# A new hand-written step order for a fused linear-attention and gated-FFN kernel: the same steps, another list

## The chip, the cores and the metric

The kernel runs on one core of one Trainium2 chip. The metric is the device time of one execution in microseconds, the median of several executions. The engines are TensorE (PE, with its weight loads shown as PEld), VectorE (DVE), ScalarE (ACT), GpSimd (POOL) and SyncE (SP, which issues DMAs).

## The reference

Eight batches of 8 heads, 576 tokens and 64 channels go through a linear attention, and the 4608 resulting rows of 512 channels go through a gated FFN, all in float32 at the interface.

```
q_s = exp(q - max(q over channels));  q_s /= sum(q_s) + 1e-9      # per token
k_s = exp(k - max(k over tokens));    k_s /= sum(k_s) + 1e-9      # per channel
kv  = einsum('bhsd,bhse->bhde', k_s, v)
x   = einsum('bhsd,bhde->bhse', q_s, kv)      # then laid out as [4608, 512]
out = ((x @ w1) * (x @ w2)) @ w3 @ w_out      # w1, w2: 512x1024; w3: 1024x1024; w_out: 1024x512
```

## The kernel before

The product w3 @ w_out is formed once on the chip ("fold"), so that the FFN is two up-projections, a product, and one down-projection with the folded matrix W3O. All matmuls are in float16 with float32 accumulation. Each batch b gives 512 rows to chunk b of the FFN and 64 rows to a ninth chunk (c = 8), the tail. The first two chunks are cut into two halves of 256 rows so that the FFN can start earlier.

The whole program is a set of named steps. `Plan.add` registers a step with the engine or engines that may run it; `Plan.run` goes through one text, `ORDER`, and emits the steps in exactly that order. Nothing is scheduled after that: each engine executes its own steps in the order in which the text names them, and semaphores hold a step until what it reads is there and the buffer that it writes is free. Where a step may run on more than one engine, the letter behind the slash chooses (A is ACT, D is DVE, P is POOL). The list is the only thing that the change touches.

The steps by name, with b the batch, c the chunk, u one of the parts of the 1024 hidden columns:

- Loads: `q.b`, `k.b`, `v.b`, `w1`, `w2`, `w3`, `wo`. Those of the first two batches and the weights are issued from POOL, except q.0; the others from SP. The loads fill buffers that alternate between two, so a load of batch b waits for the last reader of batch b-2. The first of SP's later loads, `q.2`, also waits for the landing of the load `w1.1` (the gate).
- Fold: `w3t` (8 transposes on PE), `w3T` (a copy out of PSUM), `pf` (8 matmuls in two halves), `W3O` (scaled copy). There are eight of each.
- Keys: `kmx` and `cb` (column maximum, DVE), `ksub` (POOL or DVE), `kexp` (ACT), `vc` (cast of v, POOL or ACT), `kv` (PE, 72 small matmuls), `kv2` (DVE: add epsilon, reciprocal, two multiplications out of PSUM; lines L461, L462 and L464).
- Queries: `qmx` (DVE), `qsub` (POOL or DVE), `qexp` (ACT), `qsm` (row sum, DVE, L512), `qeps` (add epsilon, ACT at L518 or DVE at L519), `qrc` (reciprocal, DVE, L523), `qn` (POOL or DVE), then `qd` (a transposing DMA issued from SP, L564), or for batch 0 `qt` and `qT` through PE.
- Attention output: `xm` (the 512 rows) and `xt` (the 64 tail rows) on PE, L582, from `kv2` and the transposed q; `xs` and `xts` scale them out of PSUM into the FFN's input x.
- FFN: `up.1` and `up.0` on PE (L726), `bs` (copy of the first product, ACT or DVE), `ab` (the elementwise product, DVE, L741), `down` on PE (L748, in the tail L763), `os` (copy out, ACT or DVE) and `st` (store, SP).
- `zero` steps: one keeps 13 matmuls of zeros on PE at the start, and the others 1, 3 or 6 by their code.

PSUM is eight banks used in rotation: a step that takes a bank waits until the copy (`bs`, `ab`, `os`, `xs`, `kv2`...) of the step that had it eight takes earlier is through. `kv`, `xm` and `xt` take two banks each.

The chain of small steps for one half p of a batch's queries reads, in the code:

```
A(("qsm", b, p), "DVE", lambda p=p: qsm(p), ...
A(("qeps", b, p), MOVES, lambda eng, p=p: qeps(p, eng), [summed], port=True, size=n1 - n0)
A(("qrc", b, p), "DVE", lambda p=p: qrc(p), [("qeps", b, p)], size=n1 - n0)
```

so that `qrc` on DVE waits for `qeps`, which may be on ACT, which waits for `qsm` on DVE.

Of the kernel before, what the change touches and what calls it, by code (L numbers as in the profile page):

```python
# [78 lines left out]
up.0.1.0.1 qsub.2.1/P up.1.1.0.2 up.0.1.0.2 bs.1.0.1/A qrc.2.0 ab.1.0.1 qexp.2.1 qsm.2.1 v.2 vc.2.1/P vc.2.0/P  # L79
bs.1.0.2/A xt.0 xts.0.1/A ab.1.0.2 xts.0.0/D qd.1.1 xm.1.1 up.1.1.0.3 qn.2.0/P up.0.1.0.3 xs.1.1.0/A  # L80
qeps.2.1/A qrc.2.1 qn.2.1/P k.3 st.0.3 xs.1.1.1/A up.1.1.1.0 up.0.1.1.0 up.1.1.1.1 kmx.2.1 cb.2 q.3 bs.1.0.3/A
bs.1.1.0/A ab.1.1.0 bs.1.1.1/A up.0.1.1.1 ab.1.1.1 up.1.1.1.2 bs.1.1.2/A st.0.0 ab.1.0.3 qd.2.1 ksub.2.1/P
kexp.2.1 up.0.1.1.2 down.1.0 up.1.1.1.3 up.0.1.1.3 kmx.3.0 qmx.3.0 st.0.1 os.1.0/A ab.1.1.2 qmx.3.1 ksub.2.0/P
kexp.2.0 bs.1.1.3/A down.1.1 os.1.1/A ab.1.1.3 kv.2 qsub.3.0/P qsub.3.1/P qexp.3.0 down.1.2 os.1.2/A kv2.2
qd.2.0 xm.2.1 xs.2.1.0/A xm.2.0 xs.2.0.1/A xs.2.0.0/A down.1.3 qsm.3.0 kmx.3.1 xs.2.1.1/A up.1.2.0.0
up.0.2.0.0 up.1.2.0.1 v.3 cb.3 vc.3.0/P ksub.3.0/P qeps.3.0/A qexp.3.1 os.1.3/A bs.2.0.0/A qsm.3.1 ab.2.0.0
ksub.3.1/P qeps.3.1/A qrc.3.1 up.0.2.0.1 up.1.2.0.2 up.0.2.0.2 up.1.2.0.3 up.0.2.0.3 up.1.2.0.4 up.0.2.0.4
bs.2.0.1/A bs.2.0.2/A q.4 qmx.4.0 ab.2.0.1 kexp.3.0 ab.2.0.2 qmx.4.1 bs.2.0.3/A ab.2.0.3 qn.3.1/P qrc.3.0
qn.3.0/P qsub.4.0/P qsub.4.1/P bs.2.0.4/A k.4 ab.2.0.4 st.1.0 kexp.3.1 kmx.4.1 q.5 v.4 st.0.2 st.1.3 vc.4.1/P
up.1.2.0.5 up.0.2.0.5 up.1.2.0.6 bs.2.0.5/A vc.3.1/A ab.2.0.5 bs.2.0.6/A up.0.2.0.6 ab.2.0.6 xt.1 qd.3.1  # L90
qd.3.0 kmx.4.0 xts.1.0/A kv.3 up.1.2.0.7 bs.2.0.7/A up.0.2.0.7 st.1.1 k.5 qexp.4.0 qexp.4.1 xts.1.1/A v.5 q.6
ab.2.0.7 down.2.0 os.2.0/A kv2.3 cb.4 st.2.0 st.1.2 qmx.5.1 qsm.4.0 down.2.1 down.2.2 xm.3.0 xs.3.0.1/D
os.2.1/A os.2.2/A xm.3.1 xs.3.1.1/A xs.3.0.0/A xs.3.1.0/A down.2.3 os.2.3/A qsm.4.1 qmx.5.0 up.1.3.0.0 kmx.5.1
qeps.4.1/A qrc.4.1 bs.3.0.0/A up.0.3.0.0 ksub.4.1/P qeps.4.0/A ksub.4.0/P ab.3.0.0 up.1.3.0.1 up.0.3.0.1
up.1.3.0.2 bs.3.0.1/A ab.3.0.1 qrc.4.0 qsub.5.1/P vc.4.0/P kexp.4.0 kexp.4.1 k.6 up.0.3.0.2 up.1.3.0.3
bs.3.0.3/A bs.3.0.2/A kmx.5.0 cb.5 ab.3.0.2 up.0.3.0.3 ab.3.0.3 up.1.3.0.4 up.0.3.0.4 up.1.3.0.5 bs.3.0.4/A
bs.3.0.5/A vc.5.0/A qexp.5.1 up.0.3.0.5 ab.3.0.5 ab.3.0.4 up.1.3.0.6 bs.3.0.6/A up.0.3.0.6 up.1.3.0.7 ab.3.0.6
vc.5.1/A xt.2 qn.4.1/P qn.4.0/P qsub.5.0/P kv.4 qd.4.0 qd.4.1 xts.2.1/A bs.3.0.7/A qexp.5.0 kv2.4 up.0.3.0.7
ab.3.0.7 down.3.0 qmx.6.0 ksub.5.1/P ksub.5.0/P os.3.0/A kexp.5.1 kexp.5.0 xts.2.0/D qsm.5.0 qsm.5.1 q.7
down.3.1 qeps.5.0/A os.3.1/A qrc.5.0 qeps.5.1/D down.3.2 os.3.2/A xt.3 xts.3.0/A xts.3.1/A kmx.6.1 qrc.5.1  # L100
kv.5 kv2.5 xm.4.1 xs.4.1.0/A kmx.6.0 cb.6 xm.4.0 xs.4.0.0/A xs.4.0.1/A down.3.3 xs.4.1.1/A up.1.4.0.0
up.0.4.0.0 up.1.4.0.1 bs.4.0.1/A bs.4.0.0/A up.0.4.0.1 up.1.4.0.2 qn.5.0/P ab.4.0.0 qmx.6.1 st.2.1 v.6 st.2.3
st.3.0 st.2.2 k.7 qd.5.0 qn.5.1/P qsub.6.0/P qexp.6.0 st.3.1 qd.5.1 os.3.3/A qmx.7.0 st.3.2 up.0.4.0.2
up.1.4.0.3 up.0.4.0.3 bs.4.0.3/A ab.4.0.3 ab.4.0.1 bs.4.0.2/D ab.4.0.2 up.1.4.0.4 up.0.4.0.4 up.1.4.0.5
bs.4.0.5/D up.0.4.0.5 bs.4.0.4/A ab.4.0.4 v.7 st.3.3 up.1.4.0.6 bs.4.0.6/A up.0.4.0.6 up.1.4.0.7 up.0.4.0.7
ab.4.0.6 ab.4.0.5 bs.4.0.7/D ab.4.0.7 down.4.0 down.4.1 ksub.6.1/P qsub.6.1/P qexp.6.1 qsm.6.1 kmx.7.1
kexp.6.1 ksub.6.0/P kexp.6.0 os.4.0/D os.4.1/A down.4.2 os.4.2/A st.4.2 st.4.0 st.4.1 xt.4 xts.4.1/A qmx.7.1
vc.6.1/P vc.6.0/P qeps.6.1/A xts.4.0/A qrc.6.1 qsub.7.0/P qn.6.1/P kv.6 xm.5.1 xm.5.0 xs.5.0.0/D kv2.6
xs.5.0.1/A xs.5.1.1/A down.4.3 xs.5.1.0/A up.1.5.0.0 up.0.5.0.0 up.1.5.0.1 up.0.5.0.1 up.1.5.0.2 os.4.3/A
bs.5.0.1/A qsub.7.1/P bs.5.0.2/A kmx.7.0 cb.7 qsm.6.0 qeps.6.0/A qexp.7.0 up.0.5.0.2 up.1.5.0.3 bs.5.0.0/D  # L110
up.0.5.0.3 ab.5.0.2 up.1.5.0.4 ab.5.0.0 qrc.6.0 bs.5.0.3/A ab.5.0.3 ab.5.0.1 qexp.7.1 bs.5.0.4/A ksub.7.0/P
vc.7.0/P qn.6.0/P ksub.7.1/P kexp.7.1 up.0.5.0.4 ab.5.0.4 qd.6.0 qd.6.1 up.1.5.0.5 bs.5.0.5/D up.0.5.0.5
up.1.5.0.6 bs.5.0.6/D up.0.5.0.6 ab.5.0.6 ab.5.0.5 up.1.5.0.7 up.0.5.0.7 bs.5.0.7/D ab.5.0.7 down.5.0 down.5.1
qsm.7.1 qsm.7.0 os.5.0/D kexp.7.0 xm.6.1 xs.6.1.1/A xm.6.0 down.5.2 down.5.3 os.5.1/A qeps.7.1/A xs.6.1.0/D
qrc.7.1 qeps.7.0/D xs.6.0.0/D xt.5 xt.6 qrc.7.0 xts.5.1/D xts.6.1/D os.5.3/D xts.5.0/D xs.6.0.1/A vc.7.1/A
kv.7 kv2.7 os.5.2/A up.1.6.0.0 bs.6.0.0/D up.0.6.0.0 ab.6.0.0 up.1.6.0.1 bs.6.0.1/D xts.6.0/A up.0.6.0.1
ab.6.0.1 up.1.6.0.2 up.0.6.0.2 up.1.6.0.3 st.5.1 up.0.6.0.3 qn.7.1/P qd.7.1 qn.7.0/P qd.7.0 st.5.3 st.4.3
st.5.0 bs.6.0.2/D ab.6.0.2 bs.6.0.3/D ab.6.0.3 xm.7.1 xs.7.1.0/A xm.7.0 xs.7.0.1/D xs.7.1.1/A xs.7.0.0/A xt.7
xts.7.1/D up.1.6.0.4 up.0.6.0.4 up.1.6.0.5 bs.6.0.4/A ab.6.0.4 bs.6.0.5/A up.0.6.0.5 up.1.6.0.6 up.0.6.0.6
ab.6.0.5 xts.7.0/D bs.6.0.6/D ab.6.0.6 up.1.6.0.7 up.0.6.0.7 up.1.7.0.0 bs.6.0.7/A ab.6.0.7 down.6.0 down.6.1  # L120
up.0.7.0.0 bs.7.0.0/A os.6.1/A up.1.7.0.1 down.6.2 ab.7.0.0 bs.7.0.1/D down.6.3 os.6.0/D os.6.3/D os.6.2/A
st.6.0 st.6.1 st.5.2 st.6.2 up.0.7.0.1 up.1.7.0.2 up.0.7.0.2 up.1.7.0.3 ab.7.0.1 bs.7.0.2/D ab.7.0.2
up.0.7.0.3 up.1.7.0.4 bs.7.0.3/D up.0.7.0.4 up.1.7.0.5 up.0.7.0.5 ab.7.0.3 bs.7.0.4/D ab.7.0.4 bs.7.0.5/D
ab.7.0.5 up.1.7.0.6 up.0.7.0.6 up.1.7.0.7 bs.7.0.6/D ab.7.0.6 bs.7.0.7/A up.0.7.0.7 ab.7.0.7 down.7.0 down.7.1
down.7.2 os.7.2/A st.7.2 os.7.0/D os.7.1/D st.7.1 st.6.3 up.1.8.0.0 up.0.8.0.0 bs.8.0.0/D ab.8.0.0 up.1.8.0.1
bs.8.0.1/D up.0.8.0.1 up.1.8.0.2 ab.8.0.1 up.0.8.0.2 up.1.8.0.3 bs.8.0.2/A ab.8.0.2 up.0.8.0.3 up.1.8.0.4
up.0.8.0.4 bs.8.0.4/D ab.8.0.4 up.1.8.0.5 up.0.8.0.5 bs.8.0.3/D bs.8.0.5/A ab.8.0.3 up.1.8.0.6 bs.8.0.6/A
up.0.8.0.6 up.1.8.0.7 ab.8.0.6 bs.8.0.7/D up.0.8.0.7 ab.8.0.7 ab.8.0.5 down.7.3 os.7.3/D st.7.3 st.7.0
# [741 lines left out]
```

## Time and profile before

| | before |
|---|---|
| median of 3 runs | 235.85 us (235.81 to 236.25) |
| the profiled execution's own time | 236.41 us |
| its span | 234.6 us |
| PE busy | 228.0 us, 97% of the span |
| DVE busy | 185.7 us, 79% |
| POOL busy | 115.7 us, 49% |
| ACT busy | 112.8 us, 48% |
| HBM traffic | 38.80 MB read, 9.44 MB written |

The span is counted from the first to the last instruction of the profiled execution; its own time has 1.8 us around it, and it stands 0.56 us above the median of the unprofiled runs. A PE that is busy is not a PE at its peak, because matmuls overlap and their ends are modelled; the distance from one start to the next tells more. A wait is put down to the event that came last.

### The profile page before, as it was taken

How to read it: one execution, taken by the hardware profiler on the slowest of the kernel's cores; microseconds unless marked ns; L12 is line 12 of the kernel's file. 1: busy time of each engine (PE TensorE's matmuls, PEld its weight loads, DVE VectorE, ACT ScalarE, POOL GpSimd, SP SyncE). 2: the span in 40 equal slices, each digit the busy share in tenths (PEclk: the TensorE clock that was granted, in tenths of full speed). 3: DMA queues.
4: the chain of work that ended last, by engine and by line, in shares of the span. 5: the costliest groups of instructions: out<-in, count | busy, mean ns of one | idle time of the engine just before them, and what ended most of it. 6: DMA issues, size and time to landing. Idle time of an engine off the chain costs nothing.

```text
span 234.6 us, 4828 instructions
## 1 busy us (share of the span) xinstructions
PE 228.0 (97%) x1938; PEld 119.6 (51%) x1938; DVE 185.7 (79%) x310; ACT 112.8 (48%) x178; POOL 115.7 (49%) x77
## 2 busy tenths in 40 slices
...
GB/s 221 215 293 224 305 243 243 389 274 276 273 298 334 398 373 187 252 402 332 42 218 396 268 236 229 91 25 79 70 183 30 0 36 145 0 6 129 3 75 193
DMA packets 38358, 46.84 MB, mean 200 GB/s; under 512 B 18368, under 2 KB 21824, under 8 KB 38336
## 3 DMA queue, kind: packets, MB, share of 16 engines
...
HBM read 38.80 MB, written 9.44 MB: 206 GB/s over the span
## 4 chain that ended last, share of the span: by engine, by line
PE 89%; DMA 9%; POOL 1%; issue 0%; ACT 0%; POOLq 0%
PE pab L726 53%; PE po L748 24%; DMA w<-in_moe_w_dram 9%; PE pf L347 3%; PE po L763 3%; PE pkv L443 2%; PE xm L582 2%; PE w3t L337 1%; PE xt L582 1%; POOL w L305 0%; PE pkv L452 0%; POOL ident masks.py:199 0%; ACT osb L223 0%; POOL ident masks.py:197 0%; POOLq masks.py:199 0%
## 5 line engine op out<-in xcount | busy, mean ns | idle before, releaser
L726 PE MATMUL pab<-x,w2sb 128*128 128x512 f16 (+1 forms) x320 | 64.9, 337 | 0.0
L726 PE MATMUL pab<-x,w1sb 128*128 128x512 f16 (+1 forms) x320 | 64.9, 337 | 0.0
L741 DVE TENSOR_TENSOR ab<-pab,bsb 128x512 f16<-128x512 f32 x72 | 47.7, 682 | 16.8 <-PE pab L726 15.2
L748 PE MATMUL po<-W3O,ab 128*128 128x512 f16 x256 | 58.4, 379 | 0.0
L223 ACT CAST bsb<-pab 128x512 f16<-128x512 f32 x49 | 28.0, 584 | 49.5 <-PE pab L726 49.3
L726 PEld LDWEIGHTS <-w1sb 128*128 128x128 f16 x352 | 34.3, 98 | 27.7
L726 PEld LDWEIGHTS <-w2sb 128*128 128x128 f16 x352 | 34.1, 98 | 28.1 <-issue 0.2
L417 POOL TENSOR_TENSOR k<-k,cb 128x1152 f32<-128x1152 f32 x13 | 34.0, 2628 | 19.2 <-DVE q L486 10.3
L748 PEld LDWEIGHTS <-ab 128*128 128x128 f16 x256 | 24.4, 98 | 30.0 <-issue 2.3
L530 POOL TENSOR_TENSOR en<-eq,qr 128x1024 f16<-128x1024 f16 (+1 forms) x14 | 29.6, 2125 | 16.7 <-ACT qr L518 10.5
L378 DVE TENSOR_REDUCE km<-k 128x128 f32<-128x1152 f32 x14 | 30.3, 2167 | 0.0
L223 ACT COPY osb<-po 128x512 f32<-128x512 f32 (+2 forms) x26 | 14.7, 564 | 28.7 <-PE po L748 17.6
L486 POOL TENSOR_TENSOR q<-q,qm 128x1280 f32<-128x1280 f32 (+1 forms) x13 | 27.8, 2144 | 0.9 <-DVE qm L480 0.9
L480 DVE TENSOR_REDUCE qm<-q 128x16 f32<-128x1024 f32 (+2 forms) x16 | 21.2, 1331 | 3.8 <-DMA q<-in_q_dram 3.8
L494 ACT ACTIVATE eq<-q 128x1024 f16<-128x1024 f32 (+2 forms) x16 | 18.7, 1169 | 9.4 <-DVE q L486 8.5
L512 DVE TENSOR_REDUCE qr<-eq 128x16 f32<-128x1024 f16 (+2 forms) x16 | 21.3, 1340 | 0.2 <-ACT eq L494 0.2
L425 ACT ACTIVATE ek<-k 128x1152 f16<-128x1152 f32 x16 | 18.1, 1161 | 6.2 <-POOL k L417 6.2
L223 DVE CAST bsb<-pab 128x512 f16<-128x512 f32 x23 | 15.8, 687 | 6.4 <-PE pab L726 6.1
L227 ACT ACTIVATE x<-xm 128x512 f16<-128x512 f32 x27 | 14.4, 600 | 12.5 <-PE xm L582 12.5
L347 PE MATMUL pf<-wosb,w3T 128*128 128x512 f16 x64 | 15.6, 379 | 0.4 <-DMA wosb<-in_moe_w_out_dram 0.4
L223 DVE COPY osb<-po 128x512 f32<-128x512 f32 (+1 forms) x12 | 7.8, 654 | 9.0 <-PE po L748 4.6
L223 ACT COPY w3T<-w3t 128x1024 f16<-128x1024 f16 x8 | 8.1, 1011 | 5.3 <-PE w3t L337 4.1
...
## 6 DMA issues: line engine op xcount, KB each, us to landing
...
```

The source lines that it names most:

```text
L223: return [(nc.scalar.copy if eng == "ACT" else engine[eng].tensor_copy)(out=out, in_=in_)]
L347: nc.tensor.matmul(st["pf", ft], lhsT=st["w3T", ft][:, gt, :], rhs=wosb[:, gt, :], start=(gt == 0), stop=(gt == N_FT - 1))
L378: dve.tensor_reduce(out=st["km", b][:, two(hp), :], in_=kb[:, two(hp), :, :].rearrange("p h j d -> p h d j"), axis=AX.X, op=ALU.max)
L417: return [engine[eng].tensor_tensor(out=kb[:, two(hp), :, :], in0=kb[:, two(hp), :, :], in1=st["cb", b][:, two(hp), None, :].broadcast_to( ...
L480: dve.tensor_reduce(out=st["qm", b][:, hs, j], in_=qb[:, hs, j, :], axis=AX.X, op=ALU.max, **({"negate": True} if (b, p) in FEXP else {}))
L486: return [engine[eng].tensor_tensor(out=qb[:, hs, j, :], in0=qb[:, hs, j, :], in1=st["qm", b][:, hs, j, None].broadcast_to([P, nh, n, D]), ...
L494: nc.scalar.activation(out=st["eq", b, p], in_=qb[:, hs, j, :], func=AF.Exp)
L512: dve.tensor_reduce(out=st["qr", b][(slice(None), *part(p))], in_=st["eq", b, p], axis=AX.X, op=ALU.add)
L530: return [engine[eng].tensor_tensor(out=st["en", b][:, j, hs, :].rearrange("p j h d -> p h j d"), in0=st["eq", b, p], in1=st["qr", b][:, h ...
L726: nc.tensor.matmul(st["p", one, c, sub, u][:, a * (t1 - t0):(a + 1) * (t1 - t0)], lhsT=w[:, ct, fb * P:(fb + 1) * P], rhs=x()[:, ct, t0:t1 ...
L741: dve.tensor_tensor(out=st["ab", c][:, nf * u:nf * u + nf, t0:t1], in0=cut(st["p", 0, c, sub, u]), in1=cut(st["bsb", c, sub, u]), op=ALU.mult)
L748: nc.tensor.matmul(st["po", c, tb], lhsT=st["ab", c][:, ft, tb * P:(tb + 1) * P], rhs=W3O[:, ft, :], start=(ft == 0), stop=(ft == N_FT - 1))
```

## The change

`ORDER` is replaced by another list of the same steps. No step is added or taken out, no function differs, and every `zero` code is used as often as before (28 zero matmuls in both). Two things differ: the place of steps within each engine's own sequence, and the engine of some steps that may run on several.

- Engines: `bs` moves to ACT for 13 more of the 72 (62 on ACT and 10 on DVE, from 49 and 23). Of the 14 casts `vc`, POOL has 4 and ACT 10, from 9 and 5. DVE has 2 `w3T`, 1 `W3O`, 10 `os`, 4 `xs`, 5 `xts`, 6 `qeps` and 4 `qn`, from 0, 4, 12, 5, 7, 3 and 2.
- Loads from POOL: the same sequence, except that three neighbouring pairs are exchanged (w3.3 and w3.4, w3.6 and w3.0, w3.1 and w3.2) and w2.0 comes ahead of w2.1. Loads from SP: q2 k2 v2 q3 q4 k3 v3 k4 q5 v4 k5 q6 v5 k6 q7 v6 k7 v7 instead of q2 k2 v2 k3 q3 v3 q4 k4 q5 v4 k5 v5 q6 k6 q7 v6 k7 v7.
- PE: the same matmuls in blocks of the same sizes; the places of fold blocks in the first 33 us, of the blocks `xt`, `kv` and `xm` between the FFN's, and of some `down` blocks differ.

The core of the diff, cut to the stretches that are spoken of below:

```diff
-pf.4.1 W3O.4/D w3.0 w3t.0 W3O.3/D w3T.6/A pf.6.0 qt.0.1.0 w3T.0/A qT.0.1.0/A qt.0.1.4 pf.6.1 qT.0.1.4/A
-W3O.6/A pf.0.0 k.0.1 kmx.0.1 k.0.0 w3.7 w3t.7 w3T.7/A pf.0.1 W3O.0/A w3.5 w3t.5 pf.7.0 w3T.5/A w3.1 w3t.1
-pf.7.1 pf.5.0 pf.5.1 kmx.0.0 cb.0 ksub.0.0/D w3.2 w3t.2 w3T.1/A ksub.0.1/D kexp.0.0 pf.1.0 v.0 kv.0.0 kexp.0.1
-kv.0 W3O.5/D w3T.2/A W3O.7/A pf.1.1 kv2.0 xm.0.0 xs.0.0.0/A xm.0.1 xs.0.1.0/A xs.0.1.1/A xs.0.0.1/A pf.2.0
...
-v.1 ksub.1.0/P kexp.1.0 vc.1.1/A up.0.0.0.2 up.0.0.1.3 qn.1.0/P up.0.0.0.3 ab.0.0.2 ab.0.1.2 ab.0.0.3 down.0.0
-down.0.1 ab.0.1.3 q.2 qmx.2.0 qsub.1.1/P qexp.1.1 qsm.1.1 vc.1.0/P kv.1.0 kv.1 kv2.1 os.0.0/A os.0.1/A
-qeps.1.1/A qrc.1.1 qmx.2.1 qsub.2.0/P qexp.2.0 qsm.2.0 down.0.2 os.0.2/D qd.1.0 xm.1.0 xs.1.0.1/A xs.1.0.0/A
-qn.1.1/P k.2 kmx.2.0 down.0.3 up.1.1.0.0 os.0.3/A bs.1.0.0/A qeps.2.0/A up.0.1.0.0 ab.1.0.0 up.1.1.0.1
...
+w3t.6 w3T.6/A qT.0.0.0/A qt.0.1.0 qT.0.0.4/D qT.0.1.0/A pf.0.0 pf.6.0 qt.0.1.4 k.0.1 kmx.0.1
+k.0.0 kmx.0.0 pf.0.1 cb.0 w3.7 w3t.7 pf.6.1 ksub.0.0/D w3T.7/A pf.7.0 w3.5 W3O.6/A qT.0.1.4/A W3O.0/A w3t.5
+w3T.5/A ksub.0.1/D pf.7.1 W3O.7/A w3.2 w3t.2 pf.5.0 pf.5.1 w3.1 w3T.2/A w3t.1 pf.2.0 v.0 kexp.0.0 kv.0.0
+kexp.0.1 kv.0 pf.2.1 W3O.2/A W3O.5/D w3T.1/D pf.1.0 kv2.0 xm.0.1 xs.0.1.0/A xs.0.1.1/A pf.1.1 W3O.1/A xm.0.0
...
+q.1.1 qmx.1.1 bs.0.0.3/A bs.0.0.2/A ab.0.0.2 ab.0.0.3 down.0.0 v.1 ab.0.1.2 ab.0.1.3 ksub.1.0/P kexp.1.0
+qn.1.0/P q.2 qmx.2.0 qsub.1.1/P qexp.1.1 qsm.1.1 vc.1.1/A qeps.1.1/A qrc.1.1 down.0.1 os.0.1/A os.0.0/A
+vc.1.0/P kv.1.0 kv.1 kv2.1 down.0.2 os.0.2/A qd.1.0 xm.1.0 xs.1.0.1/A xs.1.0.0/A down.0.3 qsub.2.0/P qexp.2.0
+qn.1.1/P qmx.2.1 qsub.2.1/P k.2 kmx.2.1 up.1.1.0.0 up.0.1.0.0 up.1.1.0.1 up.0.1.0.1 os.0.3/A bs.1.0.0/A
+qsm.2.0 up.1.1.0.2 ab.1.0.0 qexp.2.1 qsm.2.1 bs.1.0.1/A qeps.2.0/A ab.1.0.1 v.2 xt.0 xts.0.0/D qeps.2.1/D
...
+st.2.1 kmx.5.1 kmx.5.0 qsub.5.1/P ksub.4.0/P os.2.3/A bs.3.0.0/A bs.3.0.1/A kexp.4.1 kexp.4.0 k.6 ab.3.0.0
+up.0.3.0.3 qeps.4.0/D qrc.4.1 up.1.3.0.4 cb.5 ab.3.0.1 qrc.4.0 bs.3.0.2/A bs.3.0.3/A qn.4.1/P qn.4.0/P
+ab.3.0.3 qexp.5.0 bs.3.0.4/A up.0.3.0.4 ab.3.0.4 ab.3.0.2 vc.4.0/A up.1.3.0.5 bs.3.0.5/A st.1.2 ksub.5.0/P
+ksub.5.1/P up.0.3.0.5 ab.3.0.5 up.1.3.0.6 up.0.3.0.6 qmx.6.0 xt.2 qd.4.0 qd.4.1 bs.3.0.6/A ab.3.0.6 qexp.5.1
```

114 lines of the change are left out of this document (55 added, 59 removed).

## The prediction

> **What bounds the kernel now.** I read the page first, then PE's waits, then the chain that ended last.
>
> ```profile
> span 234.6 us, 4828 instructions
> ...
> PE 228.0 (97%) x1938; PEld 119.6 (51%) x1938; DVE 185.7 (79%) x310; ACT 112.8 (48%) x178; POOL 115.7 (49%) x77
> ```
>
> ```profile
> PE w3t L337 <- DMA w<-in_moe_w_dram: 1.7, 3, 0.9
> PE zero L254 <- DVE zero L248: 1.6, 1, 1.6
> PE pf L347 <- DMA wosb<-in_moe_w_out_dram: 0.4, 1, 0.4
> ```
>
> ```profile
> 40.00:60.00 20.00, 20.00 (x223) 14.38 (x221) 18.38 (x26) 13.86 (x21) 15.79 (x9) 1.00 1.00 306
> ...
> 80.00:100.00 20.00, 20.00 (x175) 9.14 (x174) 19.64 (x37) 13.64 (x23) 17.01 (x8) 1.00 0.91 285
> ```
>
> PE's waits are a few at the very start, for the zeros that fill it and for the first loads; in the later windows (second and third figures: the window's length, PE's busy time) PE is busy from end to end. The chain agrees: behind the start it is PE alone.
>
> ```profile
> 22.84 0.71 PE w3t L337 x8
> 23.55 0.86 PE pf L347 x4
> ...
> 33.81 13.97 PE pab L726 x128
> 47.78 3.45 PE po L748 x16
> 51.23 0.73 PE pkv L443 x72
> 51.97 1.83 PE po L748 x8
> 53.80 0.34 PE xm L582 x8
> ...
> 224.75 6.96 PE po L763 x48
> 231.72 0.02 issue
> 231.74 0.27 ACT osb L223
> ```
>
> Four matmuls of 512 columns take 0.86 us, and the FFN's first 128 of 256 columns 13.97. So from 22.84 us, when the first w3 block that PE had to wait for is there, to the last output copy at 231.74 us, PE is the clock. A new order that keeps the matmuls can gain only ahead of that point, or in the tail; anywhere between it can only keep PE fed or starve it. The time is therefore: before, less what the start gains, plus every stall that the new list brings. Both are a few tenths; about 0.2%, 0.47 us, is what a measurement of this kernel can tell from no change.
>
> **The start.** At 22.84 us PE still has, in the old list, `w3t.5` and then `pf.7.0`, `w3t.1`, `pf.7.1` and the rest of the fold.
>
> ```profile
> 21.18 1.01 ACT L223 COPY w3T<-w3t 128x1024 f16<-128x1024 f16 x1 [1.22 <-PE w3t L337]
> 22.84 0.71 PE L337 MATMUL w3t<-ident,w 128*128 128x128 f16 x8 [0.89 <-DMA w<-in_moe_w_dram]
> 26.78 2.22 ACT L425 ACTIVATE ek<-k 128x1152 f16<-128x1152 f32 x2
> ```
>
> The 0.89 us of idle before 22.84 is what can be had. The new list has `pf.7.0` (0.86 us) ahead of `w3t.5`. It needs `w3T.7`, whose copy ends at 21.18 + 1.01 = 22.19, so it runs from about 22.3 to 23.15, and `w3t.5`, whose load comes at the same place in the queue, starts 0.3 us late with 0.86 us less behind it: 0.55 gained. The new list takes back 0.1: `xm.0.0` and `xm.0.1` stand apart, one more switch between full and quartered matmuls, and the first `up` follows them with only one `pf` half between, so that it waits for the copies of x. I take 0.45: the first `up`, at 33.81 in the chain, comes at about 33.35. The bounds are 0 (the two `kexp`, ending at 29.0, are reached no earlier) and 0.89.
>
> **The wait that takes it back.** The next place where two lists differ and PE has no room is `kv2.1`, DVE's small chain that `xm.1.0` reads.
>
> ```profile
> 50.10 1.22 DVE L480 TENSOR_REDUCE qm<-q 128x16 f32<-128x1024 f32 x1 [0.99 <-DMA q<-in_q_dram]
> ...
> 50.63 1.22 ACT L223 COPY osb<-po 128x512 f32<-128x512 f32 x2
> ...
> 51.23 1.48 DVE L512 TENSOR_REDUCE qr<-eq 128x20 f32<-128x1280 f16 x1
> ...
> 52.63 0.22 DVE L461 TENSOR_SCALAR rc<-pkv 128x2 f32<-128x2 f32 x2
> 52.75 0.31 ACT L518 ACTIVATE qr<-qr,epst 128x20 f32<-128x20 f32 x1 [0.89 <-DVE qr L512]
> ...
> 53.09 0.49 DVE L464 TENSOR_TENSOR kv<-pkv,rc 128x128 f16<-128x128 f32 x2
> ...
> 53.50 0.27 DVE L523 RECIPROCAL qr<-qr 128x20 f32<-128x20 f32 x1
> ...
> 53.73 0.41 PE L582 MATMUL xm<-qT,kv 64*64 64x256 f16 x8
> ```
>
> Read as one chain: DVE sat idle until q of batch 2 landed (50.10, `qmx.2.0`), then `qsm.1.1` from 51.23 to 52.71, then `kv2.1` from 52.63 to 53.58, then `xm.1.0` at 53.73, 0.15 us behind it. In the old list `qrc.1.1` (53.50) comes after `kv2.1`. In the new list `qrc.1.1` comes before it, and `qrc.1.1` waits for `qeps.1.1`, which stays on ACT and waits for `qsm.1.1`. `qmx.2.0` still stands ahead of all of them, and the load `q.2` stands behind the same gate with the same bytes ahead, so 50.10 stays. Step by step:
>
> - `qsm.1.1` ends at 51.23 + 1.48 = 52.71;
> - `qeps.1.1` on ACT, 52.75 to 53.06, as now;
> - `qrc.1.1` on DVE 0.03 later (the row at 14.75 below follows its `qeps`, 14.41 + 0.31 = 14.72, by so much), 53.09 to 53.36;
> - `kv2.1` starts 0.08 before that end, as 53.50 stands to 53.58 now, and takes 0.95: 53.28 to 54.23.
>
> So `kv2.1` is 0.65 us later than before, while PE, 0.45 early, would want it at 53.73 - 0.45 = 53.28. What PE makes of a `kv2` that comes late is shown by batch 0:
>
> ```profile
> 30.80 0.49 DVE L464 TENSOR_TENSOR kv<-pkv,rc 128x128 f16<-128x128 f32 x2
> 31.20 0.78 PE L582 MATMUL xm<-qT,kv 64*64 64x256 f16 x16
> ```
>
> `xm.0.0` started 0.09 before `kv2.0` ended (its first weights need only the first half), and the rest waited for the second half. So `xm.1.0` comes into its stride between 54.14 and 54.29: 0.41 to 0.56 later than the 53.73 of before. I take 0.55, since seven of its eight matmuls wait for the end. This stall swallows whatever the start gained, up to 1.0 us and any stall of the same size ahead of it: `vc.1.1`, moved behind `qexp.1.1` on ACT, may hold `kv.1` for some tenths, and they are inside the 1.0.
>
> That DVE doesn't pass a waiting instruction is shown here:
>
> ```profile
> 13.12 0.67 PE L555 MATMUL qtp<-ident,en 128*128 128x128 f16 x9
> ...
> 14.41 0.31 ACT L518 ACTIVATE qr<-qr,epst 128x18 f32<-128x18 f32 x1
> ...
> 14.75 0.27 DVE L523 RECIPROCAL qr<-qr 128x18 f32<-128x18 f32 x1 [0.85 <-ACT qr L518]
> 14.94 0.36 DVE L223 COPY qT<-qtp 128x512 f16<-128x512 f16 x1
> ```
>
> The copy at 14.94 had its input from 13.8 on, and DVE stood 0.85 us idle behind a reciprocal. The Trainium skill, TensorE: Matmul & The Clock Gate, under "Architectural detail", says the same as a rule: PE may pull weight loads ahead, while ScalarE's and VectorE's queues are strictly first in, first out. By that rule the 0.55 stands; were DVE free to take `kv2.1` first, the sum would be the start's gain alone.
>
> Queued behind the waiting instructions: on DVE `kv2.1` and `qmx.2.1`; on ACT, behind `qeps.1.1`, the copies `os.0.1` and `os.0.0`, which had run at 50.6, and `os.0.2`. At some 0.6 each (1.22 for two) the three take from 53.06 until about 54.8 and the two `xs.1.0` until 56.0. `up.1.1.0.0`, which needs both the `xs` and the bank of `os.0.0`, comes at 56.36 after 1.73 us of `down.0.3`. Nothing further is lost there.
>
> **Behind it.** `xt.0` and `xm.1.1` stand one `up` earlier than before, and they need the transposed q of `qd.1.1`.
>
> ```profile
> 56.21 1.93 SPq L564 DMA_TRANSPOSE qT<-en  x1
> ...
> 61.15 0.26 PE L582 MATMUL xt<-qT,kv 64*64 64x64 f16 x8
> ```
>
> ```profile
> qT<-en SPq DMA_TRANSPOSE x14, 4.5
> ```
>
> At the median 4.5 us to landing it is there at 60.7. PE, 0.55 late and one `up` (13.97 / 16 = 0.87) early, asks at 61.15 + 0.55 - 0.87 = 60.83. I take 0.05, with 0 and 0.5 as bounds, since a transposing DMA behind loads can take longer than the median.
>
> From there to the tail I find no second place as clear. The groups of small matmuls between the FFN's are of the same kinds in both lists. Moving 13 `bs` from DVE (0.69 each) to ACT (0.58) relieves the busier engine, but mostly in the last chunks, where DVE has room already; the relief is worth 0. In chunks 2 and 3, where DVE is the full engine (19.64 of 20 us), the DVE work listed ahead of the last `ab` of a chunk, counted with the durations of before, is at most 0.6 us more. The exchanged loads (q.3 and q.4 ahead of k.3) bring k.3 later, but `kmx.3` comes later on DVE too. The tail, `down.8.1` to the last store, has the same steps; that `down.7.3` no longer covers `ab.8.0.7` costs 0, because that product is needed only by the eighth matmul of `down.8.0`, 1.5 us on, and takes 0.69. Bounds for all of this: nothing is gained, since PE had no idle time there, and up to 1.0 us is lost.
>
> **The sum.** The start's -0.45 counts for nothing once `kv2.1` holds PE: +0.55 there, +0.05 at `xt.0`, 0 behind it: +0.6 us. The profiled execution would go from 236.41 to 237.0, its span from 234.6 to 235.2. It stood 0.56 above the median of the unprofiled runs; on that median, 235.85, the forecast is 236.45 us.
>
> **The rivals.**
>
> *The start's gain survives (faster).* If q of batch 2 landed 1.0 us earlier, by 49.1, `kv2.1` would be through when PE asks for it at 53.28, and the whole 0.45 would stay: 235.4 us; if the start takes back nothing, 235.3. For it: PE would ask for everything earlier, and SP issues the transposes and k.2 earlier, so that the DMA queues are filled otherwise. Against it: the 0.99 us of DVE idle before 50.10 shows that the landing, and not DVE, set that time, and nothing ahead of that load is taken out. The point from which it decides is 49.6: with the landing half a microsecond earlier PE loses what it gained, and the time is that of before.
>
> *Nothing that can be measured.* The same landing by some 0.3 to 0.7 us earlier, or `xm.1.0` starting by the lower bound of 0.41 with nothing behind it: 235.6 to 236.3 us.
>
> *A second stall (slower still).* The new list puts both `kmx.5`, `cb.5` and four `ab` or reciprocals ahead of `ab.3.0.2` on DVE, which frees the bank that `up.0.3.0.6` takes.
>
> ```profile
> L378 DVE TENSOR_REDUCE km<-k 128x128 f32<-128x1152 f32 x14 | 30.3, 2167 | 0.0
> ```
>
> The two column maxima alone are 4.3 us. I count `ab.3.0.2` through 0.3 us before PE asks for its bank; a DVE that runs 1.0 us later than I count (k.5 landing late, POOL's `ksub.4.0` holding `kexp.4.0` and the `bs` behind it on ACT) makes a stall of 0.7 there: 237.15 us.
>
> **How the numbers follow.** Forecast 0.46, the gain that survives 0.17, nothing measurable 0.15, a second stall 0.22. A tenth of the forecast's own case and a seventh of the faster one lie within 0.2%. Faster by over 0.2%: 0.15. Within: 0.15 + 0.05 + 0.02 = 0.22. Slower: 0.41 + 0.22 = 0.63. The forecast's own range is 236.2 to 236.9. The range for 8 in 10 reaches from the faster rival, 235.3, to a second stall at its upper bound, 237.4 (0.6 + 1.0 above the median).
>
> **What would show it.** In the profile of the changed kernel: the first `up` (L726) at about 33.35 in the chain; DVE idle until 50.1 before a `qmx`; the order L512, L523, L461 on DVE around 52 to 54, with some 0.4 us of idle before the L523 put down to ACT's L518; and PE, for the first time behind the start, idle or stretched for about a microsecond before the `xm` block at 54.2. The last output copy at about 232.3. It is wrong if that `xm` block starts at 53.4 or earlier, if PE waits there for something other than `kv2`, or if a larger gap stands in PE's later starts.

## The result, and the profile after

The changed kernel takes 236.61 us (median of 8 runs, 236.42 to 236.89) against 235.84 us (median of 8, 235.80 to 236.25). The medians stand 0.77 us apart; the ratio on record is 1.0022, with a 95% interval of 1.0012 to 1.0032, which is +0.5 us. The forecast was 236.45, or +0.6. The profiled execution took 236.65 us.

The head of the page after:

```profile
span 234.8 us, 4827 instructions
...
PE 228.8 (97%) x1938; PEld 119.9 (51%) x1938; DVE 177.4 (76%) x296; ACT 124.7 (53%) x199; POOL 105.7 (45%) x70
```

DVE lost 8.3 us of work and ACT gained 11.9, and the time got no shorter. PE's waits of after show what it got instead (total, number, longest):

```profile
PE zero L254 <- DVE zero L248: 1.6, 1, 1.6
PE xm L582 <- DVE kv L464: 0.7, 1, 0.7
PE pf L347 <- DVE w3T L223: 0.5, 1, 0.5
PE pf L347 <- ACT w3T L223: 0.3, 1, 0.3
```

The waits for weights that stood here before (1.7 us) are gone, and for the first time PE waits behind the start, at an `xm`, for `kv2`. The chain that ended last now leaves PE there (start, length, what):

```profile
32.52 0.34 PE xm L582 x8
32.86 8.85 PE pab L726 x80
41.74 0.26 ACT bsb L223
41.99 7.67 DMA q<-in_q_dram
49.69 1.22 DVE qm L480
50.91 1.40 DVE qr L512
52.33 0.32 ACT qr L518
52.68 0.28 DVE qr L523
...
53.28 0.30 DVE kv L464
53.63 0.61 PE xm L582 x8
...
232.05 0.27 ACT osb L223
```

Before, PE held the chain from 22.84 us to the last copy. Now the load of q of batch 2 and the small steps of batch 1 behind it set 12 us of it. In the chain the first `up` comes at 32.86 instead of 33.81; in the timeline the `xm` block comes at 53.63, hardly ahead of the 53.73 of before. The timeline of after at that place:

```profile
50.82 1.48 DVE L512 TENSOR_REDUCE qr<-eq 128x20 f32<-128x1280 f16 x1
...
52.33 0.31 ACT L518 ACTIVATE qr<-qr,epst 128x20 f32<-128x20 f32 x1 [2.00 <-DVE qr L512]
...
52.68 0.28 DVE L523 RECIPROCAL qr<-qr 128x20 f32<-128x20 f32 x1 [0.38 <-ACT qr L518]
52.87 0.16 DVE L461 TENSOR_SCALAR rc<-pkv 128x2 f32<-128x2 f32 x2
...
53.28 0.49 DVE L464 TENSOR_TENSOR kv<-pkv,rc 128x128 f16<-128x128 f32 x2
...
53.63 0.61 PE L582 MATMUL xm<-qT,kv 64*64 64x256 f16 x8 [0.70 <-DVE kv L464]
```

This is the order L512, L518, L523, L461 that the prediction wrote out; DVE stands 0.38 us idle ahead of the reciprocal, and PE 0.70 us ahead of `xm.1.0`. Everything is about 0.4 us earlier than forecast, because in this execution the load of q landed at 49.66 us and not at 50.08.

### The profile page after: what moved, and what is told of

Its sections match the earlier page's. It is cut to its first block, busy times and chain, and to the rows that moved or that the text cites. A ratio compares the mean times of both kernels' runs of the same rounds, so it can differ in the third digit from the quotient of the medians.

```text
span 234.8 us, 4827 instructions
## 1 busy us (share of the span) xinstructions
PE 228.8 (97%) x1938; PEld 119.9 (51%) x1938; DVE 177.4 (76%) x296; ACT 124.7 (53%) x199; POOL 105.7 (45%) x70
## 4 chain that ended last, share of the span: by engine, by line
PE 88%; DMA 5%; DVE 5%; ACT 1%; issue 0%; ACTq 0%
PE pab L726 51%; PE po L748 22%; PE pf L347 6%; DMA q<-in_q_dram 5%; PE po L763 3%; PE pkv L443 2%; PE xm L582 2%; DVE qm L480 2%; DVE q L486 1%; DVE qr L512 1%; PE w3t L337 1%; ACT w3T L223 1%; PE xt L582 1%; PE pkv L452 0%; DVE w3T L223 0%
## 5 line engine op out<-in xcount | busy, mean ns | idle before, releaser
L223 ACT CAST bsb<-pab 128x512 f16<-128x512 f32 x62 | 35.4, 587 | 58.9 <-PE pab L726 58.7
L741 DVE TENSOR_TENSOR ab<-pab,bsb 128x512 f16<-128x512 f32 x72 | 47.1, 682 | 15.1 <-PE pab L726 7.3
L530 POOL TENSOR_TENSOR en<-eq,qr 128x1024 f16<-128x1024 f16 (+1 forms) x12 | 25.0, 2088 | 22.8 <-DVE qr L523 10.6
L486 POOL TENSOR_TENSOR q<-q,qm 128x1280 f32<-128x1280 f32 (+1 forms) x13 | 27.7, 2143 | 3.3 <-DVE qm L480 3.3
L223 ACT COPY osb<-po 128x512 f32<-128x512 f32 (+2 forms) x28 | 15.5, 570 | 22.9 <-PE po L748 16.6
L512 DVE TENSOR_REDUCE qr<-eq 128x16 f32<-128x1024 f16 (+2 forms) x16 | 21.3, 1341 | 0.2 <-ACT eq L494 0.2
L223 DVE COPY osb<-po 128x512 f32<-128x512 f32 (+1 forms) x10 | 6.4, 649 | 17.2 <-PE po L748 12.9
L227 ACT ACTIVATE x<-xm 128x512 f16<-128x512 f32 x28 | 15.0, 604 | 1.9 <-PE xm L582 1.9
L223 DVE CAST bsb<-pab 128x512 f16<-128x512 f32 x10 | 6.8, 687 | 8.1 <-PE pab L726 8.0
L223 ACT CAST v<-v 128x1152 f16<-128x1152 f32 x10 | 11.6, 1168 | 0.0
```

The source lines that it names most:

```text
L223: return [(nc.scalar.copy if eng == "ACT" else engine[eng].tensor_copy)(out=out, in_=in_)]
L486: return [engine[eng].tensor_tensor(out=qb[:, hs, j, :], in0=qb[:, hs, j, :], in1=st["qm", b][:, hs, j, None].broadcast_to([P, nh, n, D]), ...
L512: dve.tensor_reduce(out=st["qr", b][(slice(None), *part(p))], in_=st["eq", b, p], axis=AX.X, op=ALU.add)
L530: return [engine[eng].tensor_tensor(out=st["en", b][:, j, hs, :].rearrange("p j h d -> p h j d"), in0=st["eq", b, p], in1=st["qr", b][:, h ...
L741: dve.tensor_tensor(out=st["ab", c][:, nf * u:nf * u + nf, t0:t1], in0=cut(st["p", 0, c, sub, u]), in1=cut(st["bsb", c, sub, u]), op=ALU.mult)
```

## The experiments

All twelve are lists of the same steps with the same arithmetic. In the profiles of the lists written for the experiments line numbers are one lower (`xm` is L581, `kv2` L463, `w3t` L336). e1 to e4 ran together on one chip, e5 to e8 and e9 to e11 likewise, and e12 by itself; the kernel before, run beside them, had medians of 236.06, 235.96, 236.09 and 236.07 us. The ratio given with each run is to the kernel before beside it.

**First: how far is the profiled before its usual self, and is it `kv2.1`?**

*e1, the kernel before, unaltered.*

> The kernel before, unchanged, profiled once more. In the profile of the changed kernel every load landed 0.4 us earlier than in the one profile of before (the first weights at 7.16 instead of 7.59 us), and q of batch 2 at 49.66 instead of 50.08. Theory 1: that is a difference between executions, not of the list; then this profile has q of batch 2 at about 49.65, xm.1.0 at about 53.3 and a span of about 234.1 us. Theory 2: the list moved the loads; then this profile repeats 50.1, 53.7 and 234.6. The time is that of before either way, ratio 1.000.

235.96 us (11 runs, 235.75 to 236.61; ratio 0.9993, 0.9985 to 1.0002). Its profile is 0.3 us shorter than the first one of before, and q of batch 2 lands at 49.73 us and `xm.1.0` starts at 53.09. So part of what seems gained between the first two profiles is a difference between two executions, and e1's profile (236.07 us) is the fairer one to compare with. Against it the profile of after has `xm.1.0` 0.54 us late and takes 0.58 us more.

*e2, one swap in the old list.*

```diff
-kv2.1 os.0.0/A os.0.1/A qeps.1.1/A qrc.1.1
+qeps.1.1/A qrc.1.1 kv2.1 os.0.0/A os.0.1/A
```

> The kernel before with one thing of the change alone: qeps.1.1 and qrc.1.1 stand ahead of kv2.1 (and of os.0.0 and os.0.1). Theory (the wait at kv2.1 is what the change loses): kv2.1 0.65 us later, xm.1.0 0.5 us later, and everything behind it by as much: +0.5 us, ratio 1.002. Rival (PE has cover there, the loss lies in the later chunks): 0.

236.54 us (11 runs, 236.28 to 237.00; ratio 1.0018, 1.0009 to 1.0026): +0.58 us on e1's median, and +0.4 by the ratio. The timeline of e1, then that of e2:

```profile
52.28 0.22 DVE L461 TENSOR_SCALAR rc<-pkv 128x2 f32<-128x2 f32 x2
...
53.09 0.61 PE L582 MATMUL xm<-qT,kv 64*64 64x256 f16 x8
```

```profile
52.77 0.28 DVE L522 RECIPROCAL qr<-qr 128x20 f32<-128x20 f32 x1 [0.38 <-ACT qr L517]
52.96 0.16 DVE L460 TENSOR_SCALAR rc<-pkv 128x2 f32<-128x2 f32 x2
...
53.72 0.61 PE L581 MATMUL xm<-qT,kv 64*64 64x256 f16 x8 [0.59 <-DVE kv L463]
```

`kv2.1` starts 0.68 us later and `xm.1.0` 0.63. This exchange alone makes a loss about as large as that of the whole new list: 1.0018 against 1.0022, with intervals that overlap.

*e3, the opposite: after with `kv2.1` put back ahead.*

```diff
-qrc.1.1 down.0.1 os.0.1/A os.0.0/A vc.1.0/P kv.1.0 kv.1 kv2.1
+down.0.1 os.0.1/A os.0.0/A vc.1.0/P kv.1.0 kv.1 kv2.1 qrc.1.1
```

> The changed kernel with one thing undone: kv2.1 ahead of qrc.1.1 on DVE, all else as changed. Theory: kv2.1 starts at the end of qsm.1.1 instead of 0.6 us later, xm.1.0 at 53.2 instead of 53.6: 0.4 to 0.55 us faster than the changed kernel, so 0.2 to 0.35 us over before (ratio 1.001). Part of the stall stays, since qsm.1.1 itself waits behind the load of q of batch 2. Rival (later chunks): as slow as the changed kernel, ratio 1.003.

A miss: 236.73 us (9 runs, 236.49 to 237.59; ratio 1.0034, 1.0022 to 1.0047), no faster than after. The wait at `xm` is gone from its profile, as meant, yet `xm.1.0` is not earlier (53.69 us), since the whole start ran 0.83 us later than in the profile of after; and from `kv.2` to `up.1.2.0.0` PE took 0.38 us more than in e1. A late start can hardly be the whole of it: the fastest of the nine runs, 236.49, is no faster than the fastest of after, 236.42. The next runs look at the start and at what lies behind `xm.1.0`.

*e4, the start alone: the new list up to `xm.0.0`, then the old one.*

> The new list up to xm.0.0, and from there the old one. The start alone. Theory: the first up comes 0.45 us earlier than before, as in the changed kernel, but xm.1.0 can't come before kv2.1, and that not before the landing of q of batch 2 plus qmx.2.0 and qsm.1.1, with only 0.15 us of room in the kernel before: nearly all of the gain is lost there, 0 to 0.15 us faster than before (ratio 0.9995). Rival (the start's gain is real and only the rest of the new list loses it): 0.45 us faster, ratio 0.998.

235.89 us (12 runs, 235.82 to 236.96; ratio 1.0004, 0.9992 to 1.0015): no gain and no loss. `kv.0.0` comes at 27.71 us, 0.23 before e1; at `kv.1` (50.87) it is 0.23 behind, since at the joint the first `up` wait for copies of x, and from `xm.1.0` (53.13) on the two profiles stay within 0.2 us of one another.

**Second: what lies behind the first wait.**

*e5, after unaltered, as a control.*

> The changed kernel unaltered, as a control on the chip of this call. Two theories of why the list with kv2.1 put back ahead of qrc.1.1 was no faster: (1) the new start hangs on when the weights land; in that execution the 9th load (w3.7) landed at 20.88 us where it had landed at 19.92 in the profile of after, and TensorE reached kv.0.0 0.83 us later, so the wait at kv2.1 was not what came last. Then this control gives about 236.6 us (ratio 1.002 to 1.003), and in its profile xm.1.0 starts at 53.6 to 53.7 whichever of the two came last: kv2.1 where w3.7 lands before about 20.1, the start where it lands after about 20.6. (2) The swap itself costs something behind xm.1.0: then this control is 0.1 us or more faster than the swapped list was (236.73), and xm.2.1 and up.1.2.0.0 lie as far behind xm.1.0 as in the first profile of after (22.85 and 25.15 us), not 0.2 more.

236.67 us (12 runs, 236.37 to 237.65; ratio 1.0026, 1.0013 to 1.0039), the same as at first. The profiled execution was the longest of them, 237.65, and its waits show what makes such a one:

```profile
PE w3t L337 <- DMA w<-in_moe_w_dram: 2.9, 3, 1.5
```

There the load w3.7 landed at 22.20 us, where it had landed at 19.92, and `xm.1.0` came at 55.00: the 53.6 to 53.7 that was expected of it, whichever came last, was too narrow. The nine profiles of lists with the new start and the five with the old one, side by side (when w3.7 and w3.5 land, and when PE starts `kv.0.0`, in us):

| start | execution | w3.7 | w3.5 | `kv.0.0` |
|---|---|---|---|---|
| old | before | 20.33 | 22.80 | 28.79 |
| old | e1 | 20.61 | 21.92 | 27.94 |
| old | e2 | 19.82 | 22.12 | 28.12 |
| old | e8 | 20.03 | 22.30 | 28.27 |
| old | e10 | 20.17 | 22.50 | 28.48 |
| new | after | 19.92 | 22.53 | 27.86 |
| new | e4 | 19.70 | 22.16 | 27.71 |
| new | e6 | 19.83 | 22.03 | 27.72 |
| new | e9 | 19.87 | 22.27 | 27.82 |
| new | e11 | 19.93 | 22.22 | 27.93 |
| new | e12 | 19.83 | 22.32 | 27.80 |
| new | e3 | 20.88 | 22.18 | 28.69 |
| new | e7 | 22.15 | 22.94 | 29.95 |
| new | e5 | 22.20 | 23.00 | 30.01 |

With the old start `kv.0.0` follows the landing of w3.5 by 5.97 to 6.02 us in all five, and `w3t.5` by 0.04 to 0.15: PE waits for it, as the prediction read, except in e1, where it landed early and PE stood without a gap there. (In e2 and e8 the profile puts this wait down to a DVE step, `kmq`.) With the new start it doesn't depend on w3.5, and stands at 27.7 to 27.9 as long as w3.7 lands by 19.9; but where w3.7 lands at 20.9 or 22.2 it follows that one by 7.8. The medians, 28.27 and 27.86, put the new start 0.41 us ahead; the means, 28.32 and 28.39, don't, because of the three late ones.

*e6, after with the first wait taken out: DVE does `qsm.1.1` while it waits for q.*

```diff
-qmx.2.0 qsub.1.1/P qexp.1.1 qsm.1.1 vc.1.1/A qeps.1.1/A qrc.1.1 down.0.1
+qsub.1.1/P qexp.1.1 qsm.1.1 qmx.2.0 vc.1.1/A qeps.1.1/A down.0.1
...
-kv.1 kv2.1 down.0.2
+kv.1 kv2.1 qrc.1.1 down.0.2
```

> After, with VectorE's qsm.1.1 ahead of qmx.2.0 (so that it fills the time in which VectorE waited for the load of q) and qrc.1.1 behind kv2.1; all other engines' lists are after's. Theory (the wait at kv2.1 is the loss): kv2.1 starts at about 52.0 us in place of 52.87, xm.1.0 needs no wait, and with loads landing as in the profile of after the time is 236.65 - 0.75 = 235.9 us; with loads landing as in the run of the swapped list, the start comes last and it stays at 236.6. A median of 236.1 to 236.3 if the executions are of both kinds. Rival (what was lost is lost over the whole list, not at kv2.1): 236.6 in every execution, with the time lost found behind xm.1.0.

A miss again, and the one that teaches most: 236.92 us (9 runs, 236.80 to 237.73; ratio 1.0040, 1.0025 to 1.0054). Here the weights landed early, `kv2.1` started at 51.70 and `xm.1.0` at 52.71 us, 0.92 before after. But PE's waits of e6 have a new row:

```profile
PE pkv L442 <- ACT ek L424: 0.6, 1, 0.6
```

and `up.1.2.0.0`, 0.92 ahead at `xm.1.0`, stands 0.31 behind after. The whole second batch of side work was late for the earlier PE: `qmx.2.0`, put behind `qsm.1.1`, ran 0.88 later, and with it, by 0.6 to 0.9, `qsub.2.0`, `qn.1.1` and the rest of POOL's row up to `ksub.2.0` and `kexp.2.0`. So e6 takes one wait out and makes another by the same edit.

*e7, the list of e6 up to `xm.1.0`, then the old one.*

> The list of the run before this one up to xm.1.0, and from there the old list. Theory: behind xm.1.0 the new list loses 0.2 us against the old one (177.53 us from xm.1.0 to the last step against 177.43 and less), so this is 0.1 to 0.3 us faster than the run before it: 235.8 to 236.1 us. It is also the version that would beat both kernels if the start gains anything: 235.8 against 235.96 for before. Rival (the new list's later part is as good as the old): equal to the run before within 0.1 us.

236.61 us (13 runs, 236.45 to 238.67; ratio 1.0024, 1.0011 to 1.0037), not the hoped 235.8. Its profile is that of its longest execution (w3.7 at 22.15), and shows a wait that the joint itself makes:

```profile
PE pab L725 <- ACT x L226: 0.9, 1, 0.9
```

The old list has `qexp.2.0` ahead of the `xs.1.0` copies on ACT, and `qexp.2.0` waits, through `qsub.2.0`, for the `qmx.2.0` that is now late. So this run doesn't tell the old later part from the new.

*e8, the old list up to `xm.1.0`, then the new one.*

> The old list up to xm.1.0 and the new one from there: the later part of the change alone, with neither the new start nor qrc.1.1 ahead of kv2.1. Theory: it loses the 0.2 us that the profile of after shows behind xm.1.0 (a wait of 0.1 us at each of a few places): 236.1 to 236.3 us. Rival (the later part costs nothing, and the forecast's step of zero for it is right): 235.96 us as before.

236.50 us (12 runs, 236.42 to 237.07; ratio 1.0021, 1.0010 to 1.0032): +0.54 on before, more than the 0.2 expected. With neither the new start nor the swap the new list loses the same half microsecond further on. The starts of steps in five profiles tell it (us):

| step | e1 (old) | e2 | after | e6 | e8 |
|---|---|---|---|---|---|
| `kv.1` | 50.64 | 50.80 | 50.63 | 50.48 | 50.95 |
| `kv2.1` | 52.28 | 52.96 | 52.87 | 51.70 | 52.25 |
| `xm.1.0` | 53.09 | 53.72 | 53.63 | 52.71 | 53.18 |
| `up.1.1.0.0` | 55.37 | 56.00 | 55.91 | 54.80 | 55.34 |
| `up.1.1.1.0` | 62.87 | 63.50 | 63.41 | 62.71 | 63.14 |
| `kv.2` | 73.40 | 74.03 | 73.94 | 73.89 | 73.68 |
| `xm.2.1` | 75.94 | 76.57 | 76.48 | 76.60 | 76.35 |
| `up.1.2.0.0` | 78.23 | 78.86 | 78.78 | 79.09 | 78.84 |
| last copy | 231.41 | 231.92 | 232.05 | 232.24 | 232.00 |

In e2 and after the loss is made between `kv.1` and `xm.1.0`, and nothing is added up to `up.1.2.0.0`. In e8 it is made in two pieces behind: 0.30 between `up.1.1.0.0` and `up.1.1.1.0`, where `xm.1.1`, one `up` earlier than in the old list, waits for the transposed q (landed 60.12, `xm.1.1` at 60.17), and 0.33 from `kv.2` to `up.1.2.0.0`. The second piece in the timelines of e1 and of e8:

```profile
74.36 0.22 DVE L461 TENSOR_SCALAR rc<-pkv 128x2 f32<-128x2 f32 x2
...
74.82 0.49 DVE L464 TENSOR_TENSOR kv<-pkv,rc 128x128 f16<-128x128 f32 x2
...
75.94 0.63 PE L582 MATMUL xm<-qT,kv 64*64 64x512 f16 x8
```

```profile
75.54 0.22 DVE L460 TENSOR_SCALAR rc<-pkv 128x2 f32<-128x2 f32 x2
...
76.01 0.49 DVE L463 TENSOR_TENSOR kv<-pkv,rc 128x128 f16<-128x128 f32 x2
76.35 0.34 PEld L581 LDWEIGHTS <-kv 64*64 64x64 f16 x8 [0.56 <-DVE kv L463]
76.35 0.82 PE L581 MATMUL xm<-qT,kv 64*64 64x512 f16 x8
```

`kv2.2` is 1.2 us later, and `xm.2` takes 0.82 us and not 0.63. A table by stage (length, then busy time of PE, PEld, DVE, ACT and POOL), first of e1, then of after:

```profile
60.00:78.00 18.00, 18.00 (x215) 12.19 (x213) 17.72 (x28) 10.95 (x20) 15.09 (x8) 1.00 1.06 325
78.00:95.00 17.00, 17.00 (x156) 8.03 (x155) 16.72 (x30) 12.05 (x20) 14.09 (x7) 1.00 0.93 296
```

```profile
60.00:78.00 18.00, 18.00 (x217) 12.46 (x216) 17.70 (x31) 12.32 (x19) 15.45 (x7) 1.00 1.07 319
78.00:95.00 17.00, 17.00 (x156) 7.99 (x155) 16.68 (x31) 13.97 (x23) 11.67 (x5) 1.00 0.95 301
```

DVE is full for 35 us, in the old list as much as in the new: what DVE lost in work it lost elsewhere. What differs is the order. In the new list DVE has `qmx.4.0` (1.2 us), `ab.1.0.1` (0.7) and two small query steps more between `qsm.2.1` and `kv2.2`.

So the later part of the new list loses 0.54 us by itself (e8), and the swap 0.4 to 0.6 by itself (e2), yet after loses no more than 0.5 to 0.8 with both. The profiles show two reasons. At `xm.2` the first loss hides the second: in after `kv2.2` ends at 76.23 us and PE asks for it at 76.48, so that a PE 0.54 earlier would have had to wait for about 0.3 of that (an estimate from these two times). At `xm.1.1` there is nothing to hide: in after the transposed q had landed at 59.08, ahead of even the 59.80 at which PE reached this place in e8. Part of this comes from the swap itself: `qrc.1.1` ahead of `kv2.1` gives POOL its `qn.1.1` 0.4 us earlier (53.03 us in after, 53.47 in e8), and with that `qsm.2.1` (59.01 against 59.44). The rest is the transposing DMA of `qd.1.1`, which took 3.7 us in after and 4.3 in e8. This goes with the list: it took 3.3 to 3.9 us in the eight profiles that have the new order around it and 4.1 to 4.6 in the six that have the old one. What in the order makes it quicker stays open.

**Third: can order take the second wait out?**

*e9, the list of e3 with `qmx.4.0` (and the `qsub.4.0` that reads it) behind `kv2.2`.*

```diff
-q.4 qmx.4.0 qmx.3.0 qsub.3.0/P qsub.4.0/P vc.2.0/A
+q.4 qmx.3.0 qsub.3.0/P vc.2.0/A
...
-kv.2 kv2.2 down.1.2
+kv.2 kv2.2 qmx.4.0 qsub.4.0/P down.1.2
```

> After with kv2.1 ahead of qrc.1.1 and with VectorE's qmx.4.0 (1.2 us, wanted only by a step of GpSimd some 5 us later) moved behind kv2.2. Theory, formed on the runs so far: the new list has two waits in a row that hide one another. The first is at kv2.1 (xm.1.0 0.55 us late). The second is at kv2.2: q of batch 2 lands, qmx.2.0, qrc.1.1, qn.1.1 and qsub.2.1 on GpSimd, qexp.2.1, qsm.2.1, and from there VectorE is busy without a gap up to kv2.2, so xm.2.1 waits. Putting kv2.1 first makes qrc.1.1 0.6 us later and so the second chain; in the run of that swap alone the four matmul groups at xm.2 took 0.30 us more than in the old list. With qmx.4.0 out of that stretch kv2.2 is 1.2 us earlier and the second wait is gone: 236.3 to 236.4 us against 236.7 for the swap alone. Rival (the second place is not what holds it, the late start is): no change, 236.7.

237.33 us (6 runs, 236.57 to 238.16; ratio 1.0049, 1.0031 to 1.0067): slower. In its profile `xm.2` is again as quick as in e1, but the microsecond of DVE work that was put off comes back in chunk 2, where `down.2.0` now waits for its last product:

```profile
94.89 0.68 DVE L740 TENSOR_TENSOR ab<-pab,bsb 128x512 f16<-128x512 f32 x1
...
95.62 0.11 PEld L747 LDWEIGHTS <-ab 128*128 128x128 f16 x2 [0.84 <-DVE ab L740]
95.62 0.39 PE L747 MATMUL po<-W3O,ab 128*128 128x512 f16 x1 [0.35 <-DVE ab L740]
```

In after the same product ran at 93.92 and nobody waited. Counted from start to start of the matmuls, the wait costs PE 0.51 us, and another behind `kv.3` 0.24. Up to `qmx.4.0` this list is e3's, here with an early start, and so it shows what e3's profile could not. Of PE's waits:

```profile
PE xm L581 <- DVE kv L463: 0.3, 1, 0.3
PE pkv L442 <- ACT ek L424: 0.2, 1, 0.2
```

`xm.1.0` comes at 53.16 us, 0.47 before after, but still behind a wait; and at `kv.2`, which waits for `kexp.2.0`, only 0.21 of that is left.

*e10, the same move in the list of e8.*

> The old list up to xm.1.0, the new one from there (236.50 us as measured), with the one change that qmx.4.0 goes behind kv2.2. Same theory, with neither the new start nor the first wait in play: its profile without this move shows the matmuls at xm.2 0.30 us slower, so 236.2 us; the other 0.27 us that it loses at xm.1.1 stay. Rival (the loss at xm.2 is not VectorE's queue): 236.5 us as before the move.

237.37 us (6 runs, 236.74 to 237.95; ratio 1.0051, 1.0032 to 1.0071). Again the wait at `xm.2` went, and 0.40 us behind `kv.3` and 0.51 at `down.2.0` came.

*e11, that move, the first wait out as in e6, and three more of chunk 1.*

The moves of chunk 1, in words:

```
+vc.2.1/A and vc.2.0/A ahead of bs.1.1.2/A
+bs.1.0.1/A ahead of qexp.2.1, ab.1.0.1 ahead of qsm.2.1
+up.0.1.0.2 ahead of xt.0
```

> After with every wait found in its chunk 1 taken out by order alone: qsm.1.1 ahead of qmx.2.0 and qrc.1.1 behind kv2.1 (first wait), qmx.4.0 behind kv2.2 (second wait), vc.2.1 and vc.2.0 ahead of bs.1.1.2 on ScalarE (kexp.2.0 ended at 73.83 us and held kv.2 0.6 us when the first wait was gone), bs.1.0.1 and ab.1.0.1 ahead of qexp.2.1 and qsm.2.1, and up.0.1.0.2 ahead of xt.0 on TensorE (xm.1.1 waited 0.14 us for qT, and an up 0.18 us for ab.1.0.1). Theory: with weights landing early kv.1 is at 50.5 us and up.1.2.0.0 follows 27.2 us after it as in the old list: 77.7 us against 78.2 (before) and 78.8 (after), so 235.5 us; where they land late, up to 236.3; median 235.5 to 235.9, faster than after by 0.8 and perhaps than before by 0.3. Rival (there is always one more floor: side work of batch 2 is as late as TensorE): 236.3 or more, with kv.2 or xm.2.1 still waiting.

237.26 us (6 runs, 237.01 to 238.20; ratio 1.0055, 1.0037 to 1.0073). In chunk 1 the moves bring less than half of what they were meant to: `kv.2` comes at 73.03 and `up.1.2.0.0` at 78.32 us, 0.46 before after where 1.1 was expected. The next to be late was a load: DVE stood 0.64 us ahead of `kmx.3.1` for k of batch 3, which the new list loads behind q of batches 3 and 4, and `kv2.2` stands behind that step. And `up.1.3.0.0` is at 101.61 where after has 101.11. All that was won before 79 us and half a microsecond more is lost in chunk 2, at the same two places as in e9.

**Fourth: give DVE less instead of later.**

*e12, the list of e11 with `qmx.4.0` back, and two DVE steps on ACT.*

The edit, the last line in words:

```diff
-xts.0.0/D
+xts.0.0/A
-qeps.2.1/D qrc.2.0 kmx.2.0 qrc.2.1 qd.1.1 xm.1.1 xts.0.1/A xs.1.1.0/A bs.1.0.2/A xs.1.1.1/A
+qrc.2.0 kmx.2.0 qd.1.1 xm.1.1 xts.0.1/A xs.1.1.0/A bs.1.0.2/A xs.1.1.1/A qeps.2.1/A qrc.2.1
+bs.1.1.3/A ahead of kexp.2.0, ab.1.1.3 behind ab.1.1.2
```

> The list of the five moves with qmx.4.0 back at its place, and VectorE relieved in that stretch by giving work away rather than putting it later: xts.0.0 (0.28 us) and qeps.2.1 (0.17 us) go to ScalarE; bs.1.1.3 and ab.1.1.3 come ahead of kexp.2.0 and kmx.3.1. Theory (VectorE's queue is full from q.2's landing to the end of chunk 2, so work that is moved behind kv2.2 comes back as waits at kv.3 and down.2.0, 0.4 and 0.5 us, as the two runs with qmx.4.0 late showed; work taken off it does not): no wait at kv.3 and at down.2.0, up.1.2.0.0 at 78.3 to 78.5 us (after 78.78, before 78.23), down.2.0 to up.1.3.0.0 again 7.57 us, and a time of 236.1 to 236.4 us, below after (236.65) and still not below before (235.96). Rival (any order of the new list meets one more wait, whatever VectorE is relieved of): 236.6 or more, the place of the new wait named by the profile.

236.34 us (12 runs, 235.91 to 236.91; ratio 1.0008, 0.9995 to 1.0020): within the expected 236.1 to 236.4, below after in its median, though the two did not run side by side, and not to be told from before. As expected there is no wait at `kv.3` or `down.2.0`, and 7.57 us from `down.2.0` to `up.1.3.0.0`. But `up.1.2.0.0` was not at 78.3 to 78.5 in the profiled execution (236.75 us, its second longest). The timeline names a load:

```profile
69.96 2.35 DVE L479 TENSOR_REDUCE qm<-q 128x16 f32<-128x1024 f32 x2 [0.42 <-DMA q<-in_q_dram]
...
75.55 0.20 DVE L460 TENSOR_SCALAR rc<-pkv 128x2 f32<-128x2 f32 x2
...
76.35 0.40 PE L581 MATMUL xm<-qT,kv 64*64 64x512 f16 x1 [0.83 <-DVE kv L463]
```

q of batch 4, which the new list loads ahead of k of batch 3, landed at 69.86 us here (68.39 in after), DVE stood 0.42 us before `qmx.4.0`, and `kv2.2` was late once more. That the faster half of its executions lacks this wait was not profiled and is not shown. No list tried here beats the kernel before.

## Why the prediction was right, and where its reasons fell short

- *PE is the clock from 22.84 us on; only the start, a stall or the tail can change the time.* Held: the differences that were followed up were found as waits of PE for a step of another engine or for a load, at the start or behind it.
- *The start gains 0.45, with `pf.7.0` filling PE's wait for w3.5.* Right in cause, and too large: with the old start `kv.0.0` follows w3.5, with the new one not, which gives 0.41 there between the medians of five and nine profiles, and 0.3 at the first `up`; e4, with the start alone, gained nothing in time. The first `up` came at 32.86 and not at 33.35 because the profiled before was an execution with a late w3.5; the 0.89 us of idle read there is not its usual size, and in e1 there was none. Unforeseen: the new start follows w3.7 instead, and loses where that one lands late. This cost the forecast little, since it counted the gain as lost.
- *`kv2.1` behind `qrc.1.1` costs 0.55 us net and swallows the start's gain.* Right: the order of the four steps is the one that was written out, `xm.1.0` is 0.54 late in after against e1, and e2, which has this exchange and nothing else, has it 0.63 late. That a gain was swallowed is not seen in that pair of profiles, which stand equal at `kv.1` (50.63 and 50.64). The rule of the Trainium skill cited there (TensorE: Matmul & The Clock Gate, "Architectural detail"), that VectorE's queue is strictly first in, first out, bore the step, and the rows agree: `kv.1` ended at 51.10 us in after, DVE was idle from 52.30 to 52.68, and `kv2.1` still came behind the reciprocal, at 52.87.
- *q of batch 2 lands at 50.1; 0.3 to 0.7 us earlier, and nothing can be measured.* It landed at 49.66, so by the prediction's own condition that rival was due, and it did not come. The condition was read off one execution: in e1 the old list has the landing at 49.73 too, and `xm.1.0` at 53.09 instead of 53.73, so the difference between the lists stayed. The forecast held because it was a difference added to the median, and not because 50.1 was right.
- *+0.05 at `xt.0`.* Nothing in after, where the transposed q had landed in time; 0.30 in e8, where it had not. The bound of 0.5 held. Only `xm.1.1` reads that q: in e8 `xt.0`, which is of batch 0, ran at 59.80, ahead of the landing.
- *0 behind `xt.0`, the rest of chunk 1, chunks 2 and 3 and the tail; DVE's relief is worth 0.* Right for the time of after: from `up.1.2.0.0` to the last copy after takes 0.09 us more than e1. The reason was too weak: at the end of chunk 1 there is the loss of 0.33 us at `kv2.2` that e8 shows, and in after the first loss hid it.
- *"Were DVE free to take `kv2.1` first, the sum would be the start's gain alone."* This sentence failed, and the prediction's own rows speak against it: `kv2.1` would still stand behind `qsm.1.1`, through at 52.71, as in the old list, where `xm.1.0` follows the end of `kv2.1` by 0.15 us; so little more than that could be gained. In e9, with `kv2.1` first and an early start, PE still waits 0.3 us there, and e3 is no faster than after. Nor was a second stall looked for that stands in for the first: the prediction priced one only as adding to it (at `ab.3.0.2`, where PE did not wait). So the faster rival had a chance too high. Even where `kv2.1` was through at 52.65, ahead of the 53.28 at which PE was to ask for it (e6), the list was slow, though there by a wait of its own edit's making.

The time was right because of the step that was worked out, and e2 shows that step alone. That undoing it does not help has a cause that the prediction did not see: steps of the next batch are nearly as late.
